# Retention on half-array tiles: two heads side by side in place of block-diagonal k and v

## The chip, the cores and the metric

The kernel runs on one core of a Trainium2 chip. The metric is device microseconds of one execution. Times are medians of the runs named. PE is the TensorE matmul engine, DVE VectorE, ACT ScalarE, POOL GpSimd; "a change of mode" means that two matmuls that follow one another on PE use array tiles of different size, such as 128*128 and 128*64 (rows*columns).

## The reference

Retention (a causal product with a decay per head, without softmax) over 8 batches, 8 heads, 576 tokens and head size 64, then a gated feed-forward network (FFN) over the 4608 tokens (shortened):

```python
def _attn_ref(q, k, v):
    B, H, S, D_ = q.shape                      # 8, 8, 576, 64
    scores = np.matmul(q, k.transpose(0, 1, 3, 2)) / np.sqrt(D_)
    gamma = 1.0 - 2.0 ** (-5.0 - np.arange(H))
    pos = np.arange(S)
    rel = pos[:, None] - pos[None, :]
    Dmat = np.where(rel >= 0, gamma[:, None, None] ** rel[None, :, :], 0.0)
    return np.matmul(scores * Dmat[None], v)

def _moe_ref(x, w_gate, w_val, w_out):         # x: 4608 x 512, d_ff 1536
    gate = 1.0 / (1.0 + np.exp(-(x @ w_gate)))
    return (gate * (x @ w_val)) @ w_out
```

## The kernel before

Each batch is cut into five steps: four of 128 tokens (full) and one of 64 (short), 40 steps in all. The decay is folded into q and k, so a step needs scores within its chunk (qk), the product of masked scores and v plus the carried state times q (pv), and the update of the state (st). The state is absent in a batch's first step, and the short step does not update it. These groups of matmuls are placed between groups of FFN matmuls (h, op) so that PE seldom rests. Heads are handled in pairs. The first nine steps (EARLY) transpose k and q on PE, the later ones by DMA. A pair of heads of size 64 fills the 128 rows of the array (tiles 128*128 in the trace), and to keep the heads apart, k and v are written block-diagonally, with zeros between:

```python
def cast_v(s):                                 # late steps; POOL
    nc.gpsimd.tensor_copy(out=vn[0:n], in_=v32[0:n])
    for j in range(n // 64):
        for hh in range(2):
            nc.gpsimd.tensor_copy(out=vb[hh * 64:hh * 64 + 64, j, :, hh * 64:hh * 64 + 64],
                                  in_=v32[j * 64:j * 64 + 64, hh::2, :])

def phase_qk(s):                               # late full steps; 4 pairs of heads (M = 4)
    ...
            nc.tensor.matmul(qkp[:, mm, 0:128], lhsT=kb[:, 0, m, :], rhs=qT[:, m, 0:128], ...)
            nc.tensor.matmul(qkp[:, mm, 128:192], lhsT=kb[:, 1, m, :], rhs=qT[:, m, 64:128], ...)

def phase_pv(s):
    for m in range(M):
        mm = []
        if c > 0:
            mm.append((state[s - 1][:, m, :], qT[:, m, 0:n], 0, n))
        ...                                    # late full step: two key blocks, 128 + 64 queries
            mm.append((vb[:, 0, m, :], pt[:, m, 0:128], 0, 128))
            mm.append((vb[:, 1, m, :], pt[:, m, 128:192], 64, 128))
        for i, (w, x, a, e) in enumerate(mm):
            nc.tensor.matmul(pvp[:, m, a:e], lhsT=w, rhs=x, start=(i == 0), stop=(i == len(mm) - 1))

def phase_st(s):                               # computes both heads' products and the cross ones
    for m in range(M):
        nc.tensor.matmul(stp[:, m, :], lhsT=ks[:, 2 * m:2 * m + 2, :], rhs=vm, ...)
```

## Time and profile before

| | kernel before |
|---|---|
| time, median of its runs | 353.05 us (351.79 to 355.98, 4 runs) |
| span of the profiled execution | 352.0 us |
| PE busy / share of the chain that ended last | 97% / 90% |
| DVE, ACT, POOL busy | 53%, 35%, 46% |
| changes of mode in the built program | 12 |

PE is busy nearly always and carries the chain, while the others have room. The lines that show it stand in the prediction. The second thing to take from the table is the last row: only the transposes, the scores and the P.V of the one early 64-token step use part of the array, so PE runs in one mode nearly from start to end.

### The profile page before, as it was taken

How to read it: one execution, taken by the hardware profiler on the slowest of the kernel's cores; microseconds unless marked ns; L12 is line 12 of the kernel's file. 1: busy time of each engine (PE TensorE's matmuls, PEld its weight loads, DVE VectorE, ACT ScalarE, POOL GpSimd, SP SyncE). 2: the span in 40 equal slices, each digit the busy share in tenths (PEclk: the TensorE clock that was granted, in tenths of full speed). 3: DMA queues.
4: the chain of work that ended last, by engine and by line, in shares of the span. 5: the costliest groups of instructions: out<-in, count | busy, mean ns of one | idle time of the engine just before them, and what ended most of it. 6: DMA issues, size and time to landing. Idle time of an engine off the chain costs nothing.

```text
span 352.0 us, 6947 instructions
## 1 busy us (share of the span) xinstructions
PE 340.2 (97%) x2573; PEld 198.8 (56%) x2607; DVE 186.1 (53%) x371; ACT 123.7 (35%) x235; POOL 160.3 (46%) x260
## 2 busy tenths in 40 slices
PE   8999799998999999999999999999999999999996
PEld 3556345876866656656656655544555555544444
DVE  4765665665758645624637765553565346503320
ACT  5444322443334424324324433332433233323321
POOL 4834573737956654643365773553475500000000
PEclk9999999999999999999999999999999999999999
DMA  9999999999989999929928999857685320011002
GB/s 175 285 274 359 259 275 212 241 233 162 182 166 224 130 198 209 180 74 154 210 75 176 162 211 193 164 69 167 170 156 80 89 76 0 2 67 52 2 29 91
DMA packets 155249, 54.85 MB, mean 156 GB/s; under 512 B 143824, under 2 KB 148176, under 8 KB 155216
## 3 DMA queue, kind: packets, MB, share of 16 engines
q1 hardware_dynamic: 155072, 54.28, 73.4%
q8 instruction: 20, 0.33, 0.4%
q10 hardware_dynamic: 144, 0.13, 0.1%
q14 instruction: 13, 0.11, 0.1%
HBM read 37.75 MB, written 9.44 MB: 134 GB/s over the span
## 4 chain that ended last, share of the span: by engine, by line
PE 90%; DVE 3%; POOL 2%; DMA 1%; issue 1%; SPq 1%; ACT 1%; DVEq 0%; ACTq 0%
PE h L446 51%; PE op L509 23%; PE pv L361 5%; PE op L630 2%; PE st L374 2%; PE qk L325 2%; DMA k<-in_k_dram 1%; PE qk L313 1%; PE idle L128 1%; SPq L80 1%; PE qk L327 1%; POOL kbd L179 1%; PE op L499 1%; DVE wv_sb L192 1%; DVE kbd L297 1%
## 5 line engine op out<-in xcount | busy, mean ns | idle before, releaser
L446 PE MATMUL h<-xT,wv_sb 128*128 128x512 bf16 (+3 forms) x591 | 117.1, 319 | 2.2 <-DVE wv_sb L192 1.8
L446 PE MATMUL h<-xT,wg_sb 128*128 128x512 bf16 (+3 forms) x595 | 117.9, 319 | 1.0 <-POOL wg_sb L190 0.4
L473 DVE TENSOR_TENSOR gv<-g,h 128x512 bf16<-128x512 bf16 (+1 forms) x106 | 66.1, 624 | 70.8 <-PE h L446 68.5
L469 ACT ACTIVATE g<-h 128x512 bf16<-128x512 f32 (+1 forms) x106 | 58.0, 547 | 103.1 <-PE h L446 81.3
L509 PE MATMUL op<-wo_sb,gv 128*128 128x512 bf16 x357 | 84.2, 379 | 0.7
L446 PEld LDWEIGHTS <-wg_sb 128*128 128x128 bf16 x600 | 53.3, 98 | 39.3 <-POOL wg_sb L190 1.2
L446 PEld LDWEIGHTS <-wv_sb 128*128 128x128 bf16 x600 | 52.2, 98 | 35.3 <-DVE wv_sb L192 3.2
L214 POOL TENSOR_TENSOR ks<-k,ktab 128x512 bf16<-128x512 f32 (+1 forms) x40 | 41.7, 1042 | 65.2 <-DMA k<-in_k_dram 20.6
L243 POOL CAST vbd<-v 64x256 bf16<-64x256 f32 x110 | 44.0, 400 | 45.2 <-PE pv L361 40.9
L509 PEld LDWEIGHTS <-gv 128*128 128x128 bf16 x372 | 34.9, 98 | 37.6
L329 DVE TENSOR_TENSOR pt<-qk,tri 128x384 bf16<-128x384 f32 x48 | 24.5, 552 | 35.6 <-PE qk L327 35.6
L481 ACT COPY ob<-op 128x512 f32<-128x512 f32 x35 | 20.3, 587 | 58.9 <-PE op L509 50.6
L224 POOL TENSOR_TENSOR qs<-q,qtab 128x512 bf16<-128x512 f32 (+1 forms) x31 | 33.0, 1064 | 0.2 <-DMA q<-in_q_dram 0.2
L362 ACT CAST xT<-pv 128x512 bf16<-128x512 f32 (+1 forms) x40 | 21.7, 543 | 28.9 <-PE pv L361 28.5
L297 DVE COPY kbd<-kT 64x512 bf16<-64x512 bf16 (+1 forms) x62 | 29.2, 472 | 1.0
L383 DVE TENSOR_TENSOR sb<-st,bdm 128x512 bf16<-128x512 f32 x32 | 22.0, 687 | 6.2 <-PE st L374 6.2
L240 POOL CAST vn<-v 128x512 bf16<-128x512 f32 (+1 forms) x31 | 19.6, 631 | 0.0
L361 PE MATMUL pv<-qT,sb 128*128 128x128 bf16 (+1 forms) x128 | 19.3, 213 | 0.0
L361 PE MATMUL pv<-pt,vbd 128*128 128x128 bf16 (+1 forms) x220 | 17.7, 204 | 0.0
L459 ACT ACTIVATE g<-h 128x256 bf16<-128x256 f32 x29 | 11.1, 384 | 18.1 <-PE h L446 16.5
L361 PEld LDWEIGHTS <-vbd 128*128 128x128 bf16 x220 | 15.0, 98 | 3.5
L128 PE MATMUL idle<-blank 128*128 128x512 bf16 x48 | 15.4, 441 | 1.3 <-DVE blank L121 1.3
(67 smaller groups left out, 229.7 us busy)
## 6 DMA issues: line engine op xcount, KB each, us to landing
out_dram<-ob SPq DMA_DIRECT2D x35, 256.0 KB, 2.2
v<-in_v_dram SPq DMA_DIRECT2D x32, 256.0 KB, 3.7
k<-in_k_dram SPq DMA_DIRECT2D x32, 256.0 KB, 4.5
q<-in_q_dram SPq DMA_DIRECT2D x32, 256.0 KB, 4.9
wg<-in_moe_w_gate_dram SPq DMA_DIRECT2D x12, 256.0 KB, 4.9
wv<-in_moe_w_val_dram SPq DMA_DIRECT2D x12, 256.0 KB, 5.5
wo<-in_moe_w_out_dram SPq DMA_DIRECT2D x12, 256.0 KB, 5.5
v<-in_v_dram SPq DMA_DIRECT2D x8, 128.0 KB, 3.2
```

Of the source, the lines that this page charges most:

```text
L214: nc.gpsimd.tensor_tensor(out=ks[0:n], in0=k32[0:n], in1=ktab[0:n, c, :].unsqueeze(2).to_broadcast([n, H, D]), op=ALU.mult)
L224: eng.tensor_tensor(out=qs[0:n], in0=q32[0:n], in1=qtab[0:n, c, :].unsqueeze(2).to_broadcast([n, H, D]), op=ALU.mult)
L243: nc.gpsimd.tensor_copy(out=vb[hh * 64:hh * 64 + 64, j, :, hh * 64:hh * 64 + 64], in_=v32[j * 64:j * 64 + 64, hh::2, :])
L297: nc.vector.tensor_copy(out=kb[p0:p0 + 64, 0:nj, :, p0:p0 + 64].rearrange("p j m t -> p m j t"), in_=kT[p0:p0 + 64, 0:M, 0:n].rearrange("p ...
L329: nc.vector.tensor_tensor(out=pt[:, 2 * g:2 * g + 2, :], in0=qkp[:, :, 0:192], in1=tri.unsqueeze(1).to_broadcast([P, 2, 192]), op=ALU.mult)
L361: nc.tensor.matmul(pvp[:, m, a:e], lhsT=w, rhs=x, start=(i == 0), stop=(i == len(mm) - 1))
L362: nc.scalar.copy(out=xT[:, :, t0:t0 + n], in_=pvp[:, :, 0:n])
L383: nc.vector.tensor_tensor(out=sb, in0=st_tiles[b], in1=bdm.unsqueeze(1).to_broadcast([P, M, P]), op=ALU.mult)
L446: nc.tensor.matmul(out, lhsT=w_sb[:, kc, fc * P:(fc + 1) * P], rhs=xT[:, kc, t0 + a:t0 + e], start=(kc == 0), stop=(kc == NKC - 1))
L469: nc.scalar.activation(out=g[:, 0:n], in_=h1[:, 0:n], func=AF.Sigmoid)
L473: nc.vector.tensor_tensor(out=gvs[some[0]][:, a:e], in0=g[:, 0:n], in1=h2[:, 0:n], op=ALU.mult)
L509: nc.tensor.matmul(opp, lhsT=gvs[fc][:, nb * P:(nb + 1) * P], rhs=wo_sb[:, fc, :], start=(fc == 0), stop=(fc == NFC - 1))
```

## The change

The intent is to drop the zeros. A head needs only 64 rows (its size) in the scores, and only 64 columns (its size) in P.V and the state. So scores of the two heads of a pair are to run on the two row halves, and P.V and the state on the two column halves, at the same time (measured below: a pair of 128 columns every 56 ns). POOL no longer casts v a second time into a block-diagonal tile, DVE no longer copies k into one, and PE multiplies fewer zeros. The core of the diff:

```diff
@@ cast_v
-            for j in range(n // 64):
-                for hh in range(2):
-                    nc.gpsimd.tensor_copy(out=vb[hh * 64:hh * 64 + 64, j, :, hh * 64:hh * 64 + 64],
-                                          in_=v32[j * 64:j * 64 + 64, hh::2, :])
@@ phase_kb and later_constants (block-diagonal k and its clearing): gone
@@ phase_qk, all steps
+        for m in range(M):
+            for hh in range(2):
+                r = slice(hh * 64, hh * 64 + 64)
+                nc.tensor.matmul(qkp[hh][0:n, m, 0:n], lhsT=kT[r, m, 0:n], rhs=qT[r, m, 0:n],
+                                 start=True, stop=True)
@@ phase_pv
         for m in range(M):
             if c > 0:
+                for hh in range(2):
+                    r = slice(hh * 64, hh * 64 + 64)
+                    nc.tensor.matmul(pvp[r, m, 0:n], lhsT=state[s - 1][:, m, r], rhs=qT[:, m, 0:n],
+                                     start=True, stop=False)
+            for hh in range(2):
+                r = slice(hh * 64, hh * 64 + 64)
+                nc.tensor.matmul(pvp[r, m, 0:n], lhsT=vn[0:n, 2 * m + hh, :], rhs=pt[0:n, hh, m, 0:n],
+                                 start=(c == 0), stop=True)
@@ phase_st
         for m in range(M):
+            for hh in range(2):
+                nc.tensor.matmul(stp[hh * 64:hh * 64 + 64, m, :], lhsT=ks[:, 2 * m + hh, :], rhs=vn[:, 2 * m + hh, :], ...)
@@ phase_sv: two copies of 64x256 instead of one masked copy of 128x512
```

More of the change, by code (lines that the diff above doesn't have):

```diff
@@ L147 @@
     nc.scalar.activation(out=warm, in_=lnscale, func=AF.Sigmoid)
-    NB = 4
-    vbd = [consts.tile([P, 2, M, P], BF16, name=f"vbd{i}") for i in range(NB)]
-    kbd = [consts.tile([P, 2, M, P], BF16, name=f"kbd{i}") for i in range(3)]
-    vpad = [consts.tile([P, M, 2, P], BF16, name=f"vpad{i}") for i in range(3)]
-    kpad = [consts.tile([P, M, 2, P], BF16, name=f"kpad{i}") for i in range(2)]
-    for i in range(3):
-        nc.vector.memset(vpad[i], 0.0)
-        if i < 2:
-            nc.gpsimd.memset(kpad[i], 0.0)
-    tri2 = consts.tile([P, P], BF16)
-    nc.gpsimd.memset(tri2, 1.0)
-    nc.gpsimd.affine_select(out=tri2, in_=tri2, compare_op=ALU.is_ge, fill=0.0, base=0,
-                            pattern=[[1, P]], channel_multiplier=-1)
-    bdm = consts.tile([P, P], BF16)
-    nc.vector.memset(bdm, 0.0)
-    nc.vector.memset(bdm[0:64, 0:64], 1.0)
-    nc.vector.memset(bdm[64:128, 64:128], 1.0)
-    tri = consts.tile([P, 192], BF16)
-    def later_constants():
-        nc.gpsimd.memset(tri, 1.0)
-        for p0 in (0, 64):
-            for c0 in (0, 128):
-                nc.gpsimd.affine_select(
-                    out=tri[p0:p0 + 64, c0:c0 + 64], in_=tri[p0:p0 + 64, c0:c0 + 64],
-                    compare_op=ALU.is_ge, fill=0.0, base=0,
-                    pattern=[[1, 64]], channel_multiplier=-1)
-        for t in kbd:
-            nc.gpsimd.memset(t, 0.0)
+    NB = 3
+    sbd = [consts.tile([P, M, P], BF16, name=f"sbd{i}") for i in range(NB)]
+    for i in range(NB):
+        nc.vector.memset(sbd[i], 0.0)
+    tri = consts.tile([P, P], BF16)
+    nc.gpsimd.memset(tri, 1.0)
+    nc.gpsimd.affine_select(out=tri, in_=tri, compare_op=ALU.is_ge, fill=0.0, base=0,
+                            pattern=[[1, P]], channel_multiplier=-1)
     wg_sb = consts.tile([P, NKC, DFF], BF16)
@@ L203 @@
     turned = {}
-    def pair_view(t, n):
-        return t[0:n].rearrange("p m a c -> p m (a c)").rearrange("p m (x c) -> p m x c", c=D)[:, :, 0::3, :]
     def cast_k(s):
@@ L231, in cast_v @@
         v32 = loaded[s][0]
-        if s < EARLY:
-            vb = vpad[s % 3]
-            eng = nc.scalar.copy if s < 4 else nc.gpsimd.tensor_copy
-            eng(out=pair_view(vb, n), in_=v32[0:n].rearrange("p (m a) d -> p m a d", a=2))
-        else:
-            vn = nat_pool.tile([P, H, D], BF16, tag="vn", name=f"vn_{s}")
-            vb = vbd[s % NB]
-            nc.gpsimd.tensor_copy(out=vn[0:n], in_=v32[0:n])
-            for j in range(n // 64):
-                for hh in range(2):
-                    nc.gpsimd.tensor_copy(out=vb[hh * 64:hh * 64 + 64, j, :, hh * 64:hh * 64 + 64],
-                                          in_=v32[j * 64:j * 64 + 64, hh::2, :])
-            natural["v", s] = vn
-        natural["vb", s] = vb
+        vn = nat_pool.tile([P, H, D], BF16, tag="vn", name=f"vn_{s}")
+        eng = nc.scalar.copy if s < 4 else nc.gpsimd.tensor_copy
+        eng(out=vn[0:n], in_=v32[0:n])
+        natural["v", s] = vn
     def cross(s):
@@ L270, in phase_tk @@
                              is_transpose=True, start=(m == 0), stop=(m == M - 1))
-        kb = kpad[s % 2]
-        nc.vector.tensor_copy(out=kb[0:64, :, 0, 0:n], in_=kT[0:64, :, 0:n])
-        nc.vector.tensor_copy(out=kb[64:128, :, 1, 0:n], in_=kT[64:128, :, 0:n])
-        turned["kb", s] = kb
+        kc = att_pool.tile([P, M, P], BF16, tag="kT", name=f"kT_{s}", bufs=4)
+        nc.vector.tensor_copy(out=kc[:, :, 0:n], in_=kT[:, :, 0:n])
+        turned["k", s] = kc
     def phase_tq(s):
@@ L288, in phase_tq, with phase_qk @@
         turned["q", s] = qT
-    def phase_kb(s):
+    def phase_qk(s):
         n = width[STEPS[s][1]]
-        nj = n // 64
-        kT = turned.pop(("k", s))
-        kb = kbd[s % 3]
-        for hh in range(2):
-            p0 = hh * 64
-            nc.vector.tensor_copy(
-                out=kb[p0:p0 + 64, 0:nj, :, p0:p0 + 64].rearrange("p j m t -> p m j t"),
-                in_=kT[p0:p0 + 64, 0:M, 0:n].rearrange("p m (j t) -> p m j t", t=64))
-        turned["kb", s] = kb
-    def phase_qk(s):
-        b, c = STEPS[s]
-        n = width[c]
-        qT, kb = turned["q", s], turned["kb", s]
-        if s < EARLY:
-            pt = att_pool.tile([P, H, P], BF16, tag="pte", name=f"pte_{s}", bufs=2)
-            for g in range(2):
-                qkp = qk_psum.tile([P, 4, P], FP32, tag="qk", name=f"qk_{s}_{g}")
-                for i in range(4):
-                    m, hh = 2 * g + i // 2, i % 2
-                    nc.tensor.matmul(qkp[0:n, i, 0:n], lhsT=kb[:, m, hh, 0:n],
-                                     rhs=qT[:, m, 0:n], start=True, stop=True)
-                nc.vector.tensor_tensor(out=pt[0:n, 4 * g:4 * g + 4, 0:n], in0=qkp[0:n, :, 0:n],
-                                        in1=tri2[0:n, 0:n].unsqueeze(1).to_broadcast([n, 4, n]), op=ALU.mult)
-            probs[s] = pt
-            return
-        pt = att_pool.tile([P, M, 192], BF16, tag="pt", name=f"pt_{s}")
-        if n == P:
-            for g in range(2):
-                qkp = qk_psum.tile([P, 2, 256], FP32, tag="qk", name=f"qk_{s}_{g}")
-                for mm in range(2):
-                    m = 2 * g + mm
-                    nc.tensor.matmul(qkp[:, mm, 0:128], lhsT=kb[:, 0, m, :], rhs=qT[:, m, 0:128],
-                                     start=True, stop=True)
-                    nc.tensor.matmul(qkp[:, mm, 128:192], lhsT=kb[:, 1, m, :], rhs=qT[:, m, 64:128],
-                                     start=True, stop=True)
-                nc.vector.tensor_tensor(out=pt[:, 2 * g:2 * g + 2, :], in0=qkp[:, :, 0:192],
-                                        in1=tri.unsqueeze(1).to_broadcast([P, 2, 192]), op=ALU.mult)
-        else:
-            qkp = qk_psum.tile([P, 4, 128], FP32, tag="qk", name=f"qk_{s}")
-            for m in range(M):
-                nc.tensor.matmul(qkp[:, m, 0:64], lhsT=kb[:, 0, m, :], rhs=qT[:, m, 0:64],
-                                 start=True, stop=True)
-            nc.vector.tensor_tensor(out=pt[:, :, 0:64], in0=qkp[:, :, 0:64],
-                                    in1=tri[:, 0:64].unsqueeze(1).to_broadcast([P, M, 64]), op=ALU.mult)
@@ new lines, in phase_qk @@
+        qT, kT = turned["q", s], turned.pop(("k", s))
+        qkp = [qk_psum.tile([P, M, P], FP32, tag="qk", name=f"qk_{s}_{hh}") for hh in range(2)]
+        for m in range(M):
[3 more added lines that the diff above has]
+                                 start=True, stop=True)
+        pt = att_pool.tile([P, 2, M, P], BF16, tag="pt", name=f"pt_{s}", bufs=2)
+        for hh in range(2):
+            nc.vector.tensor_tensor(out=pt[0:n, hh, :, 0:n], in0=qkp[hh][0:n, :, 0:n],
+                                    in1=tri[0:n, 0:n].unsqueeze(1).to_broadcast([n, M, n]), op=ALU.mult)
@@ L343, in phase_pv @@
         t0 = first_tok[s]
-        qT = turned["q", s]
+        qT = turned.pop(("q", s))
         pt = probs.pop(s)
-        vb = natural["vb", s]
+        vn = natural["v", s]
         pvp = pv_psum.tile([P, M, P], FP32, tag="pv", name=f"pv_{s}")
         for m in range(M):
-            mm = []
             if c > 0:
-                mm.append((state[s - 1][:, m, :], qT[:, m, 0:n], 0, n))
-            if s < EARLY:
                 for hh in range(2):
-                    mm.append((vb[0:n, m, hh, :], pt[0:n, 2 * m + hh, 0:n], 0, n))
-            elif n == P:
-                mm.append((vb[:, 0, m, :], pt[:, m, 0:128], 0, 128))
-                mm.append((vb[:, 1, m, :], pt[:, m, 128:192], 64, 128))
-            else:
-                mm.append((vb[:, 0, m, :], pt[:, m, 0:64], 0, 64))
-            for i, (w, x, a, e) in enumerate(mm):
-                nc.tensor.matmul(pvp[:, m, a:e], lhsT=w, rhs=x, start=(i == 0), stop=(i == len(mm) - 1))
+                    r = slice(hh * 64, hh * 64 + 64)
[5 more added lines that the diff above has]
+                                 start=(c == 0), stop=True)
         nc.scalar.copy(out=xT[:, :, t0:t0 + n], in_=pvp[:, :, 0:n])
@@ L367, in phase_st @@
             return
-        ks, vb = natural["k", s], natural["vb", s]
+        ks, vn = natural["k", s], natural["v", s]
         if c == 0:
-            st_tiles[b] = st_psum.tile([P, M, P], FP32, tag="st", name=f"st_{b}")
+            st_tiles[b] = st_psum.tile([P, M, D], FP32, tag="st", name=f"st_{b}")
         stp = st_tiles[b]
         for m in range(M):
-            vm = pair_view(vb, P)[:, m] if s < EARLY else natural["v", s][:, 2 * m:2 * m + 2, :]
-            nc.tensor.matmul(stp[:, m, :], lhsT=ks[:, 2 * m:2 * m + 2, :], rhs=vm,
-                             start=(c == 0 and m == 0), stop=(c == NC - 2 and m == M - 1),
-                             skip_group_check=True)
+            for hh in range(2):
+                nc.tensor.matmul(stp[hh * 64:hh * 64 + 64, m, :], lhsT=ks[:, 2 * m + hh, :], rhs=vn[:, 2 * m + hh, :],
+                                 start=(c == 0 and m == 0), stop=(c == NC - 2 and m == M - 1),
+                                 skip_group_check=True)
     def phase_sv(s):
@@ L381, in phase_sv @@
             return
-        sb = att_pool.tile([P, M, P], BF16, tag="sb", name=f"sb_{s}")
-        nc.vector.tensor_tensor(out=sb, in0=st_tiles[b],
-                                in1=bdm.unsqueeze(1).to_broadcast([P, M, P]), op=ALU.mult)
+        sb = sbd[s % NB]
+        for hh in range(2):
+            r = slice(hh * 64, hh * 64 + 64)
+            nc.vector.tensor_copy(out=sb[r, :, r], in_=st_tiles[b][r])
         state[s] = sb
@@ L418, in run_phase @@
                 phase_tq(s)
-            else:
-                phase_kb(s)
         elif kind == "qk":
@@ L562 @@
     phase_sv(0)
-    later_constants()
     fill(3)
@@ L631 @@
                              start=(fc == 0), stop=(fc == NFC - 1))
-        if fc < NB:
-            nc.vector.memset(vbd[fc], 0.0)
         if fc >= 6 and fc % 2 == 0:
```

## The prediction

> **What bounds the kernel now.** I read the page's busy shares first, then the chain that ended last, then the list of waits of PE, then PE's instructions in order of time.
>
> ```profile
> PE 340.2 (97%) x2573; PEld 198.8 (56%) x2607; DVE 186.1 (53%) x371; ACT 123.7 (35%) x235; POOL 160.3 (46%) x260
> PE 90%; DVE 3%; POOL 2%; DMA 1%; issue 1%; SPq 1%; ACT 1%; DVEq 0%; ACTq 0%
> PE h L446 <- DVE wv_sb L192: 1.8, 1, 1.8
> PE qk L334 <- DVE kbd L297: 1.0, 1, 1.0
> PE qk L325 <- DVE kbd L297: 0.5, 1, 0.5
> PE qk L313 <- ACT qT L287: 0.5, 2, 0.2
> ```
>
> The first line is busy time by engine, the second the chain by engine, the others PE's waits (us in total, times, longest). PE carries 90% of the chain, and its own waits sum to under 10 us, nearly all before 93 us. So a change pays only through what PE has to stream, through what lies between two of its matmuls, or through those few waits. The 44.0 us of POOL casts into vbd and 29.2 us of DVE copies into kbd, which the change deletes, lie beside PE. By the starts of PE's matmuls, from about 100 us to 349 us one follows the other at columns/2.4 GHz plus 2 to 3 ns; there is no slack, and whatever is added to PE there shows in full.
>
> A busy PE sum overstates short matmuls (their recorded ends overlap), so I price them by starts. Ordinary attention work, in one array mode:
>
> ```profile
> 150.99 0.39 PE L374 MATMUL st<-vn,ks 128*128 128x128 bf16 x4
> 151.21 3.62 PE L509 MATMUL op<-wo_sb,gv 128*128 128x512 bf16 x16
> 154.67 0.22 PE L361 MATMUL pv<-qT,sb 128*128 128x128 bf16 x1
> ...
> 155.23 2.97 PE L509 MATMUL op<-wo_sb,gv 128*128 128x512 bf16 x13
> ```
>
> Four state matmuls take 0.22 us (56 ns each), and the P.V group of 12, 1280 columns, takes 155.23 - 154.67 = 0.56 us. Weight loads hide fully, and going between attention and FFN costs nothing. Now the one place where this kernel already leaves the 128*128 mode, the 64-token step at 49.7 us (the field after the names is the array tile, rows*columns):
>
> ```profile
> 49.73 0.19 PE L361 MATMUL pv<-qT,sb 128*128 128x64 bf16 x1
> 49.86 0.23 PE L361 MATMUL pv<-pte,vpad 64*128 64x64 bf16 x2
> 50.02 0.20 PE L361 MATMUL pv<-qT,sb 128*128 128x64 bf16 x1
> 50.16 0.23 PE L361 MATMUL pv<-pte,vpad 64*128 64x64 bf16 x2
> 50.32 0.20 PE L361 MATMUL pv<-qT,sb 128*128 128x64 bf16 x1
> 50.45 0.23 PE L361 MATMUL pv<-pte,vpad 64*128 64x64 bf16 x2
> 50.62 0.20 PE L361 MATMUL pv<-qT,sb 128*128 128x64 bf16 x1
> 50.75 0.23 PE L361 MATMUL pv<-pte,vpad 64*128 64x64 bf16 x2
> 50.91 0.39 PE L630 MATMUL op<-wo_sb,gv 128*128 128x512 bf16 x1
> ```
>
> Twelve 64-column matmuls take 1.18 us. In one mode a 64-column matmul takes 29 ns (the timeline shows 8 of them in 0.24 us at 90.8 us), so 12 should take 0.35 us. The other 0.83 us falls on 8 changes of mode: 0.104 us each. The transposes at 45.5 us, 8 matmuls in 64*128 mode between FFN work, give the same: from the start of the last FFN matmul before them to the second one after is 1.09 us, against 0.88 us by columns, so 0.21 us for a change in and one out. This is the number on which I build.
>
> [...] the eight loads at 47.6 us in 128*64 mode take 106 to 113 ns against 95 to 98 ns for full loads, and their matmuls follow at 32 ns, not 29, though only 64 columns are loaded. [...]
>
> **The change part by part.** There are 40 steps: 24 full late ones (18 with state, 6 without), 7 late ones of 64 tokens, 8 full early ones (6 with state), one early of 64 tokens.
>
> *Streaming before*, from starts in the timeline. Late full: scores 0.35 us, P.V 0.56 (0.34 without state), state 0.22: 24 x 0.35 + 18 x 0.56 + 6 x 0.34 + 24 x 0.22 = 25.8 us. Late short: 7 x (0.12 + 0.24) = 2.5. Early full: scores 0.45, P.V 0.67 (0.45), state 0.22: 3.6 + 4.9 + 1.8 = 10.3. Early short, its switches taken out: 0.5. Sum 39.1 us.
>
> *Streaming after*, if the halves fully overlap: a pair of 128 columns costs 56 ns, of 64 columns 29 to 32 ns. Scores 0.22, P.V 0.45 (0.22), state 0.13; short steps 0.12 and 0.25: 24 x 0.22 + 18 x 0.45 + 6 x 0.22 + 24 x 0.13 = 18.0, then 2.6, 5.9 and 0.4. Sum 26.9 us, a saving of 12.2. If instead the loads of the two halves go one after the other, at 29 ns on row halves and 32 ns on column halves, the load sets the pace: scores 0.23, P.V of 16 matmuls 0.51, state still 0.26, short steps 0.23 and 0.51. Sum 22.4 + 5.2 + 7.5 + 0.7 = 35.9 us, a saving of 3.2. I have no view that decides, and take 8.
>
> *Mode changes.* In the built program of before I count 12, in that of after 278. Each scores, P.V and state group now stands in its own half mode between FFN groups of 128*128: some 112 groups, two changes each, less a few where groups touch. The eight 64-token steps are worse: state-times-q is 128*64 but P.V with 64 keys is 64*64, and the loop alternates them by pair, 9 changes per step instead of 2. So 266 more changes x 0.104 = 27.7 us. They are spread among FFN groups, where PE has no slack.
>
> *Waits on PE.* The copies into kbd go and scores read the transposed k directly: 1.0 + 0.5 us of waits go. At the start POOL loses 2.7 us of kbd clearing and 1.5 us of masks ahead of the first weight cast, and PE's gaps of about 0.75 us there (14.4 to 15.5 us) can absorb the early switches: another 1 us. No wait is lost twice.
>
> *Off the path.* POOL loses 44.0 us of vbd casts and ends near 112. DVE loses kbd 29.2 and the masked state copy 22.0; it gains two state copies of 64x256 (about 0.42 each, as the 128x256 copies from PSUM, 27 in all), wider masks (48 x 0.687 against 24.5, so 8.5, and 3 in short steps): near 167. Neither bound before.
>
> Sum: 354.1 + 27.7 - 8 - 1.5 - 1 = 371.3. I shade it to 370[...].
>
> **The rivals.** (1) Mode changes turn out cheap and only the saving shows: 354.1 - 12.2 - 1.5 = 340. For it: the column count really falls by a third. Against it: ten measured changes in this trace, all of the same size. (2) The halves do not overlap at all, since each needs its own load: scores 0.45, P.V 0.90, state 0.26, 54 us of streaming instead of 39, so 354 + 28 + 15 - 3 = 394. For it: nothing in this trace shows overlap. [...] (3) The relief of POOL and DVE moves the time: their queues delay scores only at 87 and 92 us, so it is worth about 2 us, inside the sum above. (4) A new wait for PSUM: scores now fill both qk buffers at once, and both must be evicted (2 x 0.69 us) before the next scores group. Groups stand more than 2 us apart, so I expect at most 1 to 2 us, near 75 us where blocks are short.
>
> **Range and chances.** With the switch price fixed and the two ways of loading, 12.2 or 3.2 saved, the sums are 367 and 376. A switch at 80 ns instead of 104 takes 6 us off. I set 361 to 379. The change must gain nearly 9 us over my most favourable sum for it to come within 2% (under 361.2), so slower is at 0.92, and faster needs rival 1.
>
> **What would show it.** Right: in the timeline of after, an FFN matmul that ends before a scores, P.V or state group stands about 0.1 us further from the group than its columns, and the same at its end; the 64-token P.V groups take over 1 us for 16 matmuls; PE still carries some 90% of the chain, with less streaming. [...] Overlap of loads shows in the state groups: 8 matmuls in 0.13 us, or in 0.26 in series. Wrong: groups of half tiles adjoining FFN groups without a gap, or PE waiting for DVE or DMA in the late stages.

## The result

The changed kernel takes 367.8 us (367.54 to 368.85, 4 runs) against 353.05 us, a ratio of 1.041 with a 95% interval of 1.034 to 1.049. (A ratio here is the mean time of one kernel's runs over that of the other's of the same rounds, so not quite the ratio of the medians.) It is slower, inside the predicted range. The page of the changed kernel, busy time by engine and the chain by engine:

```profile
PE 358.6 (98%) x2919; PEld 187.9 (51%) x2919; DVE 164.3 (45%) x332; ACT 124.5 (34%) x235; POOL 111.3 (30%) x140
PE 94%; DMA 1%; DVE 1%; SPq 1%; ACT 1%; issue 0%; POOL 0%; ACTq 0%; DVEq 0%
```

POOL fell from 160.3 to 111.3 us and DVE from 186.1 to 164.3, as worked out, and PE carries a still larger share of the chain. Neither wait for kbd is among PE's waits any more; the longest that are left are 1.3 us at the very start and 0.9 us in total for casts of q in the first 20 us. So the lost time is on PE itself. (The granted clock is 1.0 in both profiles.) PE's instructions in order of time, where state and P.V of a full step stand between output matmuls (start us, us, what, array tile, columns, count):

```profile
152.92 0.32 PE L300 MATMUL st<-vn,ks 128*64 128x64 bf16 x8
153.17 3.63 PE L434 MATMUL op<-wo_sb,gv 128*128 128x512 bf16 x16
156.73 0.25 PE L282 MATMUL pv<-qT,sbd 128*64 128x128 bf16 x2
156.81 0.22 PE L286 MATMUL pv<-pt,vn 128*64 128x128 bf16 x2
...
157.14 0.22 PE L286 MATMUL pv<-pt,vn 128*64 128x128 bf16 x2
157.30 3.63 PE L434 MATMUL op<-wo_sb,gv 128*128 128x512 bf16 x16
```

Inside the group all is well: pairs of 128 columns follow each other at 56 ns (156.81, then 157.14 six pairs later), so the two heads do run side by side, and their starts in the trace are 3 to 4 ns apart. At the edges it is not: the 16 output matmuls need 16 x 0.216 = 3.46 us, so the group could have started at 153.17 + 3.46 = 156.63 and started at 156.73. At its end the last pair starts at 157.14, streams 0.06 us, and the next output matmul starts at 157.30, another 0.1 us late. The 64-token step is where most of it adds up:

```profile
167.05 0.22 PE L282 MATMUL pv<-qT,sbd 128*64 128x64 bf16 x2
167.20 0.22 PE L286 MATMUL pv<-pt,vn 64*64 64x64 bf16 x2
167.35 0.22 PE L282 MATMUL pv<-qT,sbd 128*64 128x64 bf16 x2
...
168.09 0.22 PE L286 MATMUL pv<-pt,vn 64*64 64x64 bf16 x2
168.24 0.82 PE L371 MATMUL h<-xT,wv_sb 128*128 128x384 bf16 x4
```

Each pair of the loop over m changes the tile twice, and each change adds 0.12 us to the 0.03 us that a pair of 64 columns streams.

The next table sums this over the kernel. It is worked out from the starts of the matmuls in the two traces: the cost of a group is the stretch from where the matmul ahead of it has streamed its columns (2.4 columns per ns, plus 2.4 ns; so do matmuls of one 128*128 group follow each other in the trace of before, at 56 ns for 128 columns and 216 ns for 512) to the start of the first matmul behind it, as a median over the groups of a kind, so that a switch on either side is in it and a rare wait is not. (Of the eight early scores groups before, six have a wait or a gap in this stretch; the 0.446 is that of the two without.)

| group | count | before, us each | after, us each | difference over the kernel, us |
|---|---|---|---|---|
| scores, full step, late / early | 24 / 8 | 0.339 / 0.446 | 0.426 | +1.9 |
| P.V with state, full, late / early | 18 / 6 | 0.563 / 0.670 | 0.664 | +1.8 |
| P.V without state, full, late / early | 6 / 2 | 0.339 / 0.447 | 0.440 | +0.6 |
| state | 32 | 0.223 | 0.341 | +3.8 |
| scores, short step (late; the early one) | 7; 1 | 0.116; 0.464 | 0.338 | +1.4 |
| P.V, short step (late; the early one) | 7; 1 | 0.232; 1.176 | 1.283 | +7.5 |
| sum | | 40.0 | 57.0 | +17.0 |

PE's listed waits sum to 6.3 us before and 3.7 us after (the two on kbd, 1.5 us, are gone, and that on wv_sb fell from 1.8 to 0.6), and 17.0 - 2.6 = 14.4 us, against 13.9 us between the two profiles and 14.75 between the medians. More than half of the sum, 8.9 us, comes from the eight short steps, which stream less than a tenth of the attention's columns (3.0 of 39.1 us by the prediction's count). Where the lost time lies can also be seen by one mark in both traces: the P.V group of step 12 starts at 110.2 us before and at 109.3 after. From it to the last matmul's start are 238.4 us before and 253.2 after. Up to the mark the change pays for its switches, through larger savings in the early steps and through waits that go; the whole loss lies in the stretch where PE never waits, which holds 193 of the changed kernel's changes of mode.

### The profile page after: what moved, and what is told of

Its sections match the earlier page's. It is cut to its first block, busy times and chain, and to the rows that moved or that the text cites. A ratio compares the mean times of both kernels' runs of the same rounds, so it can differ in the third digit from the quotient of the medians. Undisturbed runs are those within 1.5% of the kernel's fastest.

```text
span 365.9 us, 7456 instructions
## 1 busy us (share of the span) xinstructions
PE 358.6 (98%) x2919; PEld 187.9 (51%) x2919; DVE 164.3 (45%) x332; ACT 124.5 (34%) x235; POOL 111.3 (30%) x140
## 4 chain that ended last, share of the span: by engine, by line
PE 94%; DMA 1%; DVE 1%; SPq 1%; ACT 1%; issue 0%; POOL 0%; ACTq 0%; DVEq 0%
PE h L371 53%; PE op L434 23%; PE pv L286 4%; PE pv L282 3%; PE qk L261 3%; PE op L554 2%; PE st L300 2%; DMA k<-in_k_dram 1%; PE idle L128 1%; SPq L80 1%; PE op L563 1%; PE op L424 1%; PE qTp L247 1%; DVE pt L265 1%; PE kTp L233 0%
## 5 line engine op out<-in xcount | busy, mean ns | idle before, releaser
L371 PE MATMUL h<-xT,wv_sb 128*128 128x512 bf16 (+3 forms) x600 | 118.8, 320 | 0.6 <-DVE wv_sb L171 0.6
L434 PE MATMUL op<-wo_sb,gv 128*128 128x512 bf16 x372 | 85.9, 380 | 0.0
L265 DVE TENSOR_TENSOR pt<-qk,tri 128x512 bf16<-128x512 f32 (+1 forms) x80 | 47.1, 630 | 68.2 <-PE qk L261 68.2
L209 POOL CAST vn<-v 128x512 bf16<-128x512 f32 (+1 forms) x36 | 22.6, 628 | 82.1 <-PE pv L286 41.9
L311 DVE CAST sbd<-st 64x256 bf16<-64x256 f32 x64 | 26.9, 420 | 4.2 <-PE st L300 3.7
L286 PE MATMUL pv<-pt,vn 128*64 128x128 bf16 (+1 forms) x320 | 24.2, 219 | 0.3
L282 PE MATMUL pv<-qT,sbd 128*64 128x128 bf16 (+1 forms) x256 | 21.4, 223 | 0.0
L282 PEld LDWEIGHTS <-sbd 128*64 128x64 bf16 x256 | 13.6, 108 | 13.1 <-issue 11.7
L286 PEld LDWEIGHTS <-vn 128*64 128x64 bf16 (+1 forms) x320 | 16.2, 108 | 4.1 <-issue 2.6
L261 PEld LDWEIGHTS <-kT 64*128 64x128 bf16 (+1 forms) x320 | 9.3, 96 | 14.4 <-issue 11.5
```

The lines of the kernel that those rows point to most:

```text
L209: eng(out=vn[0:n], in_=v32[0:n])
L265: nc.vector.tensor_tensor(out=pt[0:n, hh, :, 0:n], in0=qkp[hh][0:n, :, 0:n], in1=tri[0:n, 0:n].unsqueeze(1).to_broadcast([n, M, n]), op=AL ...
L282: nc.tensor.matmul(pvp[r, m, 0:n], lhsT=state[s - 1][:, m, r], rhs=qT[:, m, 0:n], start=True, stop=False)
L286: nc.tensor.matmul(pvp[r, m, 0:n], lhsT=vn[0:n, 2 * m + hh, :], rhs=pt[0:n, hh, m, 0:n], start=(c == 0), stop=True)
L311: nc.vector.tensor_copy(out=sb[r, :, r], in_=st_tiles[b][r])
L371: nc.tensor.matmul(out, lhsT=w_sb[:, kc, fc * P:(fc + 1) * P], rhs=xT[:, kc, t0 + a:t0 + e], start=(kc == 0), stop=(kc == NKC - 1))
```

## The experiments

My theory: a change of mode costs 0.1 us or a little more wherever it stands, the halves overlap in full, and nothing else matters. The rivals: the cost belongs to the half-array groups as such (their loads, their semaphore waits); the halves do not overlap, or do so only by the order of instructions; the relief of POOL and DVE carries part of the time. The changed kernel's own ratio, 1.0411, comes from other rounds than those below, so differences between ratios are taken times 353 us.

### The same matmuls in two passes

Only the order of P.V in a short step: all state matmuls, then all key matmuls.

```diff
+        if n == P: todo = [(kind, m) for m in range(M) for kind in ("state", "keys")]
+        else:      todo = [(kind, m) for kind in ("state", "keys") for m in range(M)]
+        for kind, m in todo:
```

> The changed kernel with the same matmuls, but in the 64-token steps all state matmuls of P.V (128*64 tiles) come before all key matmuls (64*64 tiles), so that such a step has 3 changes of array mode in P.V instead of 9: 230 in the program instead of 278. Theory (a change costs 0.1 us or a little more wherever it stands): 48 changes fewer at 0.11 to 0.12 us each, the price read for 128*64 to 64*64, take 5.3 to 5.8 us off, so about 362.3 us, and a P.V group of a 64-token step takes 0.55 to 0.6 us from start to start instead of 1.19. Rival (the cost belongs to each half-array group, its first weight load and its semaphore wait, and not to the changes inside it): the group count is unchanged, so the time stays at 367 to 368.

Measured: 363.15 us, ratio 1.0278 (1.0224 to 1.0332), and the result was wrong, with a relative error of 0.26. The time agrees with the theory, within a us of it; the fault was mine. Each state matmul kept its start flag, now with all four pairs' sums open at once. The next run keeps, in these steps, the start flag on the first state matmul of each half alone and the stop flag on the last key matmul of each half alone, changes nothing else, and is correct. So the error of 0.26 came from these flags; how was not measured.

> The two-pass order again with the start flags mended[...]. Same instructions in the same order, so the same time as there, 362 to 364 us, and now correct. A 64-token P.V group stays at 0.49 us from start to start.

```diff
-                                     start=True, stop=False, skip_group_check=True)
+                                     start=(n == P or m == 0), stop=False, skip_group_check=True)
```

Measured: correct, 362.7 us, ratio 1.0274 (1.0222 to 1.0327). Against the changed kernel that is (1.0411 - 1.0274) x 353 = 4.8 us for 48 changes, 0.10 us each. The short step's P.V in order of time:

```profile
164.50 0.32 PE L289 MATMUL pv<-qT,sbd 128*64 128x64 bf16 x8
164.75 0.31 PE L286 MATMUL pv<-pt,vn 64*64 64x64 bf16 x8
164.99 0.82 PE L374 MATMUL h<-xT,wv_sb 128*128 128x384 bf16 x4
```

The group takes 0.49 us from start to start instead of 1.19, less than the 0.55 to 0.6 expected. With the same instructions, loads and number of groups, only the changes of mode are fewer, so the first rival falls. (By the trace 0.70 us are saved per step, 0.117 per change. Changes in the loop of two matmuls at a time cost 0.114 to 0.118 us, those at the edges of these longer groups 0.093 to 0.097. Why a change behind so few matmuls costs more was not tested. Nor does a run show what fills a change.)

### Groups side by side

```diff
         elif kind == "pv":
             phase_pv(s)
+            if EARLY <= s < NS - 1:
+                phase_st(s + 1)
+                phase_qk(s + 1)
+                phase_sv(s + 1)
... (their old places in the order, between FFN groups, are dropped)
```

> The changed kernel with P.V of a step, the state of the next and the scores of the next run one after the other from step 9 on, with no FFN matmul between: 206 changes of mode instead of 278, the same matmuls. Theory: 72 changes fewer at 0.095 to 0.1 us, 7 us off, about 360.8 us. Rival (new waits: scores, state and P.V stand so close that PE waits for the eviction of their PSUM tiles): PE's waits on DVE or ACT rise and less than 4 us, or nothing, is gained.

Measured: 361.81 us, ratio 1.0250 (1.0193 to 1.0307): 5.7 us for 72 changes, 0.08 us each. PE's waits on ACT and DVE stayed as they were (0.5 us on ACT qT; 1.2 us instead of 0.6 on the cast of wv), so no new wait took the place. The theory holds, at the low side of its price.

> Both savings of changes at once, the groups side by side and P.V of the 64-token steps in two passes: 158 changes instead of 278. Theory (changes add up, wherever they stand): 120 x 0.1 = 12 us less than the changed kernel, about 355 to 356 us. Rival (the two savings overlap or bring new waits): 358 us or more.

Both edits together: correct, 356.1 us, ratio 1.0071 (1.0022 to 1.0119), 12.0 us for 120 changes, 0.10 us each. The savings add.

### Heads one after the other

```diff
-        for m in range(M):
-            for hh in range(2):
+        for hh in range(2):
+            for m in range(M):
```

in scores, state and the P.V of full steps.

> The changed kernel with the same matmuls and the same 278 changes of mode, but in scores, state and the P.V of full steps the four pairs of one head come first and then those of the other, so that neighbours stand on the same half of the array. Theory (the two heads overlap only because the instructions alternate between the halves): scores 0.45 us instead of 0.22 in 32 full steps and 0.23 to 0.26 instead of 0.13 in 8 short ones, P.V 0.90 instead of 0.45 in 24 and 0.45 instead of 0.22 in 8, state 0.26 instead of 0.13 in 32: 7.0 + 0.9 + 10.8 + 1.8 + 4.0 = 24.5 us more, 392 us. Rival (PE overlaps different halves however they are ordered, since it looks ahead): no change, 367 to 369.

Measured: 373.87 us, ratio 1.0582 (1.0529 to 1.0636), 6 us more than the changed kernel. Both expectations were wrong. Scores took 0.340 us from start to start instead of 0.330, and state 0.257 instead of 0.247: although the four pairs of one head come first in the program, PE ran them beside those of the other. Only P.V with state, eight matmuls per head, lost: 0.820 instead of 0.570. The P.V group of this kernel in order of time:

```profile
159.91 0.24 PE L282 MATMUL pv<-qT,sbd 128*64 128x128 bf16 x1
159.99 0.22 PE L286 MATMUL pv<-pt,vn 128*64 128x128 bf16 x1
...
160.15 0.25 PE L282 MATMUL pv<-qT,sbd 128*64 128x128 bf16 x2
160.21 0.25 PE L286 MATMUL pv<-pt,vn 128*64 128x128 bf16 x2
160.26 0.25 PE L282 MATMUL pv<-qT,sbd 128*64 128x128 bf16 x2
160.32 0.25 PE L286 MATMUL pv<-pt,vn 128*64 128x128 bf16 x2
160.41 0.22 PE L282 MATMUL pv<-qT,sbd 128*64 128x128 bf16 x1
```

First four slots with one matmul, then four with two (the lines of count 2 and 0.25 us), then four with one: 12 slots where a full overlap needs 8 and none 16. So by this trace the second head's first matmul started at 160.15 beside the fifth of the first head's eight, four places ahead of its turn in the program; that PE reaches about four matmuls ahead in general is my estimate from this. The extra 0.25 us x 24 = 6.0 us is nearly the whole loss. What this run also gives is the worth of the overlap: with half of it lost in P.V alone, 6 us.

### POOL's work put back

```diff
+        if s >= EARLY:
+            for j in range(n // 64):
+                for hh in range(2):
+                    nc.gpsimd.tensor_copy(out=scrap[...], in_=v32[j * 64:j * 64 + 64, hh::2, :])
```

> The changed kernel with the removed work of POOL put back: four casts of v per late full step (two per short one) into a tile that nobody reads, some 44 us of POOL work. Theory (POOL lies beside PE, its relief bought nothing): 367 to 369 us, within 0.5% of the changed kernel. Rival (the relief of POOL brought part of the time back, for instance by earlier transposes): 2 us or more slower, with PE waits on DMA or POOL near 75 to 95 us.

Measured: 368.12 us, ratio 1.0434 (1.0362 to 1.0506), so within 0.3 us of the changed kernel's median. POOL was busy for 153.6 us against 111.3, so 42 us of work put back cost nothing measurable. DVE's work (22 us net) was not put back; of what the change takes from DVE, PE's listed waits in the kernel before name kbd alone, 1.5 us.

### Changes of mode alone, in the kernel before

Nothing of the attention is touched; some output matmuls are written as two halves.

```diff
+                for r in ((slice(0, 64), slice(64, 128)) if fc in (1, 5, 9) else (slice(0, 128),)):
+                    nc.tensor.matmul(opp[r], lhsT=gvs[fc][:, nb * P:(nb + 1) * P][:, r], rhs=wo_sb[:, fc, :], ...)
```

> The kernel before, with nothing of the attention changed, but in 31 output groups three of the twelve 128*128 matmuls (the second, sixth and tenth) written as two matmuls on the column halves with 512 columns each: 186 changes of mode more, no other work. Theory (each change costs 0.093 to 0.099 us and the two halves overlap): 186 x 0.096 = 17.9 us more than the kernel before, about 371 us. Rival (the cost of the changed kernel comes from something else in its attention): within 3 us of the kernel before.

Measured: 373.8 us, ratio 1.0584 (1.0542 to 1.0625): 20.6 us for 186 changes, 0.111 us each, more than the expected 0.096. By this trace a change into the pair of halves costs 0.093 us and one out of it, behind only two matmuls, 0.120. This is the cleanest price, since the columns streamed are the same and the attention is that of before.

### The FFN in the half mode too

If only the change costs, then the FFN can join the mode of P.V and state: every h and op matmul becomes two of 64 weight columns on the two column halves. This is on top of the two passes.

```diff
+    def halves(o, lhsT, rhs, start, stop):
+        for r in (slice(0, 64), slice(64, 128)):
+            nc.tensor.matmul(o[r], lhsT=lhsT[:, r], rhs=rhs, start=start, stop=stop)
-                    nc.tensor.matmul(out, lhsT=w_sb[:, kc, fc * P:(fc + 1) * P], rhs=xT[...], ...)
+                    halves(out, w_sb[:, kc, fc * P:(fc + 1) * P], xT[:, kc, t0 + a:t0 + e], kc == 0, kc == NKC - 1)
```

> The two-pass kernel with every FFN matmul (h, op and the fillers) also written as two matmuls of 64 columns of the weight on the two column halves, so that FFN, P.V and state share the 128*64 mode: 118 changes of mode instead of 230, and 4614 matmuls instead of 2919. Theory (only the change of mode costs, two halves side by side stream like one whole matmul, as the pairs of P.V do at 56 ns): 112 changes fewer at 0.097 us, 10.9 us off the two-pass time, about 352 us. Rival (the half loads[...] or the doubled instructions slow the FFN by 3 to 4 ns for each of some 1700 pairs): 6 us of it are given back, about 358 us.

Measured: correct, 352.69 us, ratio 0.9998 (0.9928 to 1.0067), as the theory expected and against the rival. In order of time:

```profile
151.54 1.03 PE L132 MATMUL op<-wo_sb,gv 128*64 128x512 bf16 x8
152.40 0.29 PE L307 MATMUL st<-vn,ks 128*64 128x64 bf16 x8
152.52 3.62 PE L132 MATMUL op<-wo_sb,gv 128*64 128x512 bf16 x32
155.98 0.22 PE L293 MATMUL pv<-qT,sbd 128*64 128x128 bf16 x2
```

The state group now takes 0.12 us, and 32 halves of the output take 3.46 us as 16 whole matmuls did before: no gap on either side, and no cost for twice the instructions in this stretch. The state group at 0.12 us also settles how half loads go: those of the two halves overlap, or eight of them at the 32 ns seen in the kernel before (its eight 128*64 matmuls at 47.6 us) would have taken 0.26 us.

### Fewer changes still

On top of this, the early transposes are written on column halves, and the short step's P.V stays in the 128*64 mode through zeroed rows 64 to 127 of v and of the scores; only the scores leave the mode.

```diff
-            nc.tensor.matmul(kT[:, m, 0:n], lhsT=ks[0:n, 2 * m:2 * m + 2, :], rhs=ident[0:n, 0:n], is_transpose=True, ...)
+            for hh in range(2):
+                nc.tensor.matmul(kT[hh * 64:hh * 64 + 64, m, 0:n], lhsT=ks[0:n, 2 * m + hh, :], rhs=ident[0:n, 0:n], is_transpose=True, ...)
@@ cast_v and phase_qk, short steps
+            nc.gpsimd.memset(vn[n:P], 0.0)
+            nc.gpsimd.memset(pt[n:P, :, :, 0:n], 0.0)
@@ phase_pv
-                    ... lhsT=vn[0:n, 2 * m + hh, :], rhs=pt[0:n, hh, m, 0:n]
+                    ... lhsT=vn[:, 2 * m + hh, :], rhs=pt[:, hh, m, 0:n]
```

> The kernel with FFN on column halves, with the early transposes on column halves too and the 64-token P.V kept in the 128*64 mode by zeroed rows 64 to 127 of v and of the scores: 82 changes of mode instead of 118; only the scores leave the mode. Theory: 36 changes fewer at 0.095 us, 3.4 us off, about 349 us, 1% under the kernel before. Rival (in the kernel with FFN on halves PE already waited 2.1 us for the transposed q at step 9 and 1.5 us for a q copy, and getting there sooner only lengthens these waits): 351 to 353 us, with PE's waits on DMA up by what the changes save.

Two more kernels move the loads of later steps behind a step's casts and transposes, one with half tiles and one the kernel before:

```diff
         if kind == "t":
-            while done["ld"] < min(NS, s + LEAD_LOAD + 1): load(...)
             while done["cast"] < min(NS, s + LEAD_CAST + 1): cast_k(x); ...; cast_v(x)
+            while done["ld"] < min(NS, s + LEAD_LOAD + 1): load(...)
```

> The same with one more edit: a step's casts and transposes are issued ahead of the loads of later steps, so that the first transposes do not stand behind loads in SyncE's queue. Theory (the waits near 90 us come from that queue): PE's waits for qT and kT at step 9 shrink from 2 us to nearly nothing, and the time falls 1 to 3 us under the kernel without the edit, to some 347 us. Rival (those waits come from DMA bandwidth): no difference of more than 1 us, or slower since loads come later.

> A control: the kernel before with casts and transposes issued ahead of loads, and nothing else. Whatever this edit is worth without half tiles is seen here: the waits for kbd at 87 and 92 us come from DVE's queue, so theory expects within 1 us of the kernel before (352 to 354 us). If it gains as much as in the run with half tiles, that gain is not due to tiles.

Measured: 361.42 us, ratio 1.0250 (1.0202 to 1.0298), with zeroed rows; 361.66 us, ratio 1.0248 (1.0206 to 1.0291), with casts first as well; and 353.31 us, ratio 1.0011 (0.9972 to 1.005), for the control. The first expectation failed through a fault of mine, which is the first line of PE's waits of that kernel (total us, times, longest us):

```profile
PE pv L296 <- POOL pt L273: 10.4, 1, 10.4
PE qk L269 <- DMA qT<-qs: 0.3, 1, 0.3
```

I had put the zeroing of the scores on POOL, since POOL has room on average. At step 4 it stood in POOL's queue behind the casts of w_out, and PE waited 10.4 us. Casts first moved nothing in either kernel, but with a wait of 9.2 us ahead of it in the half-tile kernel that run says nothing about its own question, and it stays open there. The zeroing moved to DVE:

```diff
-            nc.gpsimd.memset(pt[n:P, :, :, 0:n], 0.0)
+            nc.vector.memset(pt[n:P, :, :, 0:n], 0.0)
```

> The last kernel with half tiles (82 changes of mode, casts first) with one fault of mine mended: the zeroing of the score rows of a 64-token step stood in POOL's queue behind the casts of w_out, and PE waited 10.4 us for it at step 4; it now stands on DVE ahead of the mask. Theory: those 9 to 10 us come back, 361.5 becomes 350 to 351.5 us, and 82 changes against 118 make it the fastest of the study, 0.5 to 1% under the kernel before. Rival (what is saved near 50 us is waited for at 70 to 95 us, where q and k arrive late by DMA): 353 us or more, PE waits on DMA or ACT near 90 us of 2 us or more.

Measured: correct, 352.44 us (349.86 to 354.26, 6 runs), ratio 0.9983 (0.9943 to 1.0023). The 9 us came back; against the kernel before, "same", and no version clearly beats it. By the traces, the stretch from the mark at step 12 to the end takes 238.0 us against 238.4 before. The part ahead of it gained 2.0 us, and there new waits have come. PE's waits of this kernel, and ACT's between 66 and 75 us:

```profile
PE qk L269 <- ACT qT L258: 2.5, 2, 2.2
```

```profile
ACT ob L418 <- DMA out_dram<-ob: 4.9, 1, 4.9
```

ACT stood 4.9 us for an output store to leave its buffer, so its copy of q came late and PE waited 2.2 us. That is the rival's prediction, in part: in the first 100 us, where DMA is busiest (a share of 1.05 of its engines up to 60 us, 0.95 from there to 100 us, 0.65 after), PE's savings seem to be waited for. That this is all that is missing is not shown.

A second cost followed the wait. This is the granted TensorE clock of this kernel's page, in 40 slices of the span:

```profile
PEclk9999999989999999999999999999999999999999
```

By the trace the clock stood at 0.5 from 74.5 to 77.9 us, from 1 us after that wait had ended. By estimate, 3.4 us at half clock cost 1.7 us of PE's time on top of the 2.2. In the FFN run's profile the clock fell to 0.5 from 92.6 to 96.0 us at the end of a wait of 2.1 us for q, and with zeroed rows on POOL from 53.2 to 63.5 us, 5 us of it after the wait of 10.4 had ended. The profiles of before and of the changed kernel, with gaps of PE up to 2.0 us, show no such drop between start and end. So in these three profiles a wait of PE, of 2.1, 2.2 and 10.4 us, cost more than its length. The mean clock of each run fits this: the last kernel's one run at 1.0 took 349.86 us and its five at 0.99 to 0.995 took 351.32 to 354.26; the FFN kernel's two at 0.999 to 1.0 took 351.3 and 351.4 and its two at 0.994 to 0.995 took 354.0 and 356.0. Whether the last kernel would beat the kernel before without its wait is not shown by one run.

## Why the prediction was right

- **The bound.** PE sets the time: the relief of POOL, put back, made 0.3 us. DVE has more PSUM copies of another shape, but PE's listed waits on DVE in the changed kernel are early ones, 2.8 us in all.
- **The price of a change.** Ten changes in the trace of before gave 0.104 us, and this price held in the changed kernel. It is 0.111 in the kernel with added changes, and 0.08 to 0.10 in those with changes removed. In the changed kernel, 57.0 us of groups less some 26.6 us that the same groups stream without changes (32 x 0.23 scores, 24 x 0.444 and 8 x 0.220 P.V, 32 x 0.120 state, 8 x 0.367 short, from the kernels where they have none, and for the scores from the starts inside the group) leave 30.4 us over 276 changes, 0.110 each. Against before, the changes added 29.4 us where I had 27.7.
- **The saving in streaming.** Here the size was off: I took 8 us, midway between full overlap (12.2) and loads in series (3.2). Full overlap was right, 39.0 - 26.6 = 12.4 us. That term is most of why the result is 367.8 and not 371.3. With 12.2 in its place the sum is 367.1. (One sum of this term is also off: the 24 late full steps after come to 17.8 us and not 18.0, so full overlap would have been 12.4, as measured.) I took the middle as an estimate, since nothing in the trace decided between the two.
- **The waits.** I gave 2.5 us for waits that go. PE's listed waits fell by 2.6 us, and the group costs less the medians, 17.0 - 14.75, leave 2.2.
- **Luck.** The measured terms give 353.05 + 29.4 - 12.4 - 2.2 = 367.8. (They close because the 2.2 is the remainder.) The errors partly cancel: 4.4 us more saved and a start 1.0 us lower, against 1.7 us more for changes and 0.3 us less for waits.
- **The shading** to 370, for cheaper changes between two half modes, had no ground: 128*64 to 64*64 costs 0.093 to 0.118 us, no less than the others. (Nor does the range's "nearly 9 us" count from my most favourable sum: it counts from 370, and from 367 it is 6.)
- **The rivals.** Cheap changes and missing overlap are excluded. A wait for PSUM is not in PE's waits.

I had counted the short steps' changes but drawn nothing from them: their P.V holds 72 of the 278 changes, 48 of these come from the loop order alone, and the two-pass run recovers 5 us by reordering.

## What to carry to other kernels

Half-array tiles do give two matmuls in the time of one here, even with a new load for each (a pair of 128 columns every 56 ns), but entering and leaving their mode cost 0.2 us per group (each change 0.09 to 0.12 us by the traces, in and out, between the modes 128*128, 64*128, 128*64 and 64*64; 64*128 next to 64*64 did not occur); so a group pays only if it saves more than this, and the late groups of 4 to 12 matmuls here, 8 to 16 after, among full-array work did not (the early full steps' scores and P.V, which streamed more before, came out even). Put matmuls of one mode together (5.7 us here), order inner loops by tile size and not by head (4.8 us here), or bring the neighbours into the same mode: an FFN on two column halves streamed as fast as on the whole array (16 pairs of 512 columns in 3.46 us, as 16 whole matmuls). Before crediting work taken off another engine, ask whether the bound engine waited for it: 42 us of POOL work put back cost nothing measurable, while one small memset at the wrong place in POOL's queue cost 10 us, and more by the lower clock that followed (0.5 for 5 us after the wait).
